# A list scheduler's walk, repeated backwards and forwards by latest times

## The chip, the cores and the metric

The kernel runs on one core of a Trainium2 chip. The metric is the device time of one execution in microseconds; less is better. The core has five engines that work side by side, each through its own queue in order: PE (TensorE, matmuls), DVE (VectorE), ACT (ScalarE), POOL (GpSimd) and SP (SyncE, which here issues all DMAs). An instruction that waits holds up everything behind it in its queue.

## The reference

Two stages, for x of shape (8, 4224, 192) and weights of shape (8, 4224, 8, 7).

```python
# 1: a causal convolution whose 7 taps are a softmax of weight_gen, per position and head (group = 24)
w = weight_gen - np.max(weight_gen, axis=-1, keepdims=True)
w = np.exp(w)
w = w / (np.sum(w, axis=-1, keepdims=True) + 1e-09)
x_pad = np.concatenate([np.zeros((B, 6, D)), x], axis=1)
x = np.einsum('bshk,bskhg->bshg', w, x_unf).reshape(B, S, D)     # x_unf: the 7 rows up to s, by head
# 2: Fourier mixing, layer norm, MLP 192 -> 768 -> 192
mixed = np.real(np.fft.fft(np.fft.fft(x, axis=1), axis=2))
u = x + mixed
un = (u - mean(u)) / np.sqrt(var(u) + 1e-06)
return u + np.maximum(un @ w_ch1, 0.0) @ w_ch2
```

## The kernel before

**Tiling.** A batch's 4224 rows are taken as 128 partitions by 33, in nine groups: eight of 4 rows a partition and one (number 8) of one row. Batch by batch the work goes through these stages, and the stages of one batch lie beside those of the next.

- *Convolution.* SP loads x (`x_sb`, L539) and the weights (`w`, L486). DVE and ACT make the softmax (maximum L488, difference L489, Exp on ACT L491, sum L493, L497, reciprocal L498, scaling L587/L594). DVE makes a product of x and one tap (`pr`, L656), and POOL adds it to `u` (L666). POOL makes a few products itself (L654). In batch 0, where PE has nothing else to do, the odd groups' products are added by PE in PSUM (`pa`, a matmul with the identity, L662), two taps of some groups are made by ACT (`wa` L616 on DVE, then L624 in pieces of 24 columns), and ACT copies the sum to `u` (L675). The products that PE adds take the three buffers of the tag `g2`, and the loads of `g` take the same buffers later.
- *First transform.* POOL folds `u` into `sm` (L680, L682), PE multiplies it (`pg`, L687), ACT copies one half (`up`, L693), DVE combines both (`gt`, L694, L697), SP writes it to DRAM (`g_d`, L700, L701).
- *Second transform.* SP reads it back in another layout (`g`, six loads a batch, L722), PE multiplies (`pp`, L732), ACT copies to `pq` (L736 to L746), PE multiplies again (`eo`, L761), ACT copies (`ot`, L766), DVE combines and adds to `u` (L767 to L771).
- *Norm.* Statistics on DVE (`bn`, `st`, L795, L796) or ACT (L800, L802), the reciprocal root `rs` (L804 to L811), the normalised `un` on ACT (L813), split into two fp16 halves `hl` (L821 on ACT, L822 and L824 on POOL or DVE), transposed by a DMA into `ht` (L830).
- *MLP.* PE multiplies with the first weights, split in fp16 halves too (`ph`, L855, five matmuls a block), ACT and DVE make the relu and its halves (`hh`, L861 to L866), PE multiplies with the second weights (`po`, L878; fp32 for the first seven groups, so that they need no split), DVE adds (L883), SP writes out (L887).
- *Preparation of the MLP's weights* w1 and w2 (rounding to fp16 halves and scales, L387 to L430, with two small matmuls `mr_w`, `me_w` L394, L397), with copies by SP (L456). Matmuls on data that are at hand (`warm_pp`, `warm_hl`, L709) stand in PE's queue where it would be idle.

**Order.** The code writes the instructions in one order, batch by batch with the stages interleaved. Before the program is compiled, `plan` sorts all five queues anew. It builds the graph of the instructions (who reads what another wrote, and which buffer of a tag each tile needs), gives each a busy time and a time to its end (`cost`), and walks: at each step it takes the lane that can issue earliest, and on it, of the instructions that can issue at that moment, the first in the written order. `HOP` is the time from an end on one engine to a start on the next. A tile takes a buffer when one of its tag's is spare, in the written order of the tiles. Then it links each queue's instructions into that order. These lines choose:

```python
at = [(t, k) for t, k in ((opens(k), k) for k in ks) if t is not None]
if at:
    now = max(free[lane], min(at)[0])
    if best is None or now < best[0]:
        best = now, lane, min(k for t, k in at if t <= now)
```

Of the kernel before, what the change touches and what calls it, by code (L numbers as in the profile page):

```python
# [12 lines left out]
F32 = mybir.dt.float32  # L13
# [11 lines left out]
DH = 97  # L25
# [26 lines left out]

LANES = {mybir.EngineType.PE: "pe", mybir.EngineType.DVE: "dve", mybir.EngineType.Activation: "act",
         mybir.EngineType.Pool: "pool", mybir.EngineType.SP: "sp"}
HOP = {"pe": 60, "dve": 33, "act": 33, "pool": 78, "sp": 26}
BYTES = {F32: 4, I32: 4, U32: 4, F16: 2}

# [12 lines left out]
def area(ap, kind):  # L70

    if kind == "psum":
        return (0, P), [(0, 1)]
    dims, base, parts, size = [list(d) for d in ap.ap], ap.offset, (0, 1), BYTES[ap.dtype]
    if kind != "dram":
        step, n = dims.pop(0)
        parts, base = ((base // step, base // step + n), base % step) if step else ((0, P), base)
    free, run = [], 1
    for step, n in dims:
        base += min(step, 0) * (n - 1)  # L80
        if n > 1 and step:
            free.append((abs(step), n))
    free.sort(reverse=True)
    while free and (free[-1][0] <= run or np.prod([n for _, n in free]) > 80):
        step, n = free.pop()
        run += step * (n - 1)
    spans = [base]
    for step, n in free:
        spans = [b + step * k for k in range(n) for b in spans]
    return parts, sorted((b * size, (b + run) * size) for b in spans)  # L90
# [18 lines left out]
def covers(a, b):  # L109

    (pa, sa), (pb, sb) = a, b
    return len(sa) == 1 and pa[0] <= pb[0] and pb[1] <= pa[1] and sa[0][0] <= sb[0][0] and sb[-1][1] <= sa[0][1]


def cost(ins, lane, reads, writes):

    count = lambda ap: int(np.prod([n for _, n in ap.ap[1:]]))
    out = writes[0]
    n = max(map(count, reads + writes))
    if lane == "pe":  # L120
        n = count(out)
        t = 2 * max(112 if 64 < n <= DH else 56, 0.846 * n) if reads[0].dtype == F32 else max(55.5, 0.4205 * n + 0.4)
        return t, t + 178
    if lane == "sp":
        if ins.opcode == "DmaTransposeAnt":
            return 1450, 2000 + 1.2 * n
        return 400, 2000 + WIRE * count(out) * BYTES[out.dtype]
    if lane == "dve":
        t = 150 + (6.27 if ins.opcode == "Reciprocal" else 1.042) * n + (60 if len(reads) == 3 and n < 512 else 0)
        return t - 83, t  # L130
    if lane == "pool":
        t = 183 + (1.92 if out.dtype == F16 else 2.13) * n
        return t - 45, t
    t = 190 + (0.833 if out.ap[-1][0] == 1 else 1.666) * n + 90 * (len(reads) - 1)
    return (t + 100, t + 90) if len(writes) > 1 else (t - 95, t)


def plan(nc, tc, homes, holds):

    ops, index = [], {}  # L140
    writers, readers, users = defaultdict(list), defaultdict(list), defaultdict(list)
    rows = defaultdict(list)
    for at, ins in enumerate(nc.cur_bb.bb.instructions):
        reads, writes = ([a.bass_ap for a in args if hasattr(a, "bass_ap")] for args in (ins.ins, ins.outs))
# [12 lines left out]
        for name, spot, w in spots:  # L157
            kind, tag, bufs = homes[name]
            if name not in users and bufs and kind != "dram":
                rows[kind, tag].append(name)  # L160
            users[name].append(k)
            if w and homes[name][0] != "psum":
                for old in (writers, readers):
                    old[name] = [(other, j) for other, j in old[name] if not covers(spot, other)]
            (writers if w else readers)[name].append((spot, k))
        for lo, hi, first in holds:
            if lo <= at < hi and first.engine == ins.engine:
                needs.setdefault(index[first.name], False)
        ops.append((ins, lane, cost(ins, lane, reads, writes), needs, {n for n, _, _ in spots}))

    after, left = defaultdict(list), [len(op[3]) for op in ops]
    for k, op in enumerate(ops):
        for j in op[3]:
            after[j].append(k)
    uses = {name: len(set(ks)) for name, ks in users.items()}
    ends, placed = defaultdict(float), set()
    spare = {row: [0.0] * homes[names[0]][2] for row, names in rows.items()}
    heads = {row: 0 for row in rows}
    ready = [0.0] * len(ops)
    free, waiting = ({lane: v for lane, v in zip(LANES.values(), vs)} for vs in ([0.0] * 5, [set() for _ in range(5)]))  # L180
    order = {lane: [] for lane in LANES.values()}

    def opens(k):

        t = ready[k]
        for name in ops[k][4]:
            row = homes[name][:2]
            if name in placed or row not in rows or not homes[name][2]:
                continue
            while rows[row][heads[row]] in placed:  # L190
                heads[row] += 1
            if rows[row][heads[row]] != name or not spare[row]:
                return None
            t = max(t, min(spare[row]) + HOP[ops[k][1]])
        return t

    for k, n in enumerate(left):
        if n == 0:
            waiting[ops[k][1]].add(k)
    table = None  # L200
    for _ in ops:
        best = None
        for lane, ks in waiting.items():
            at = [(t, k) for t, k in ((opens(k), k) for k in ks) if t is not None]
            if at:
                now = max(free[lane], min(at)[0])
                if best is None or now < best[0]:
                    best = now, lane, min(k for t, k in at if t <= now)
        now, lane, k = best
        ins, _, (busy, done), _, names = ops[k]  # L210
        if lane == "act":
            kind = str(getattr(ins, "func", "")).split(".")[-1]
            if kind in ("Exp", "Sqrt") and kind != table:
                now, table = now + 1283, kind
        waiting[lane].remove(k)
        order[lane].append(ins)
        free[lane], end = now + busy, now + done
        for name in names:
            row = homes[name][:2]
            if name not in placed:  # L220
                placed.add(name)
                if row in rows and homes[name][2]:
                    spare[row].remove(min(spare[row]))
            uses[name] -= 1
            ends[name] = max(ends[name], end)
            if not uses[name] and row in rows and homes[name][2]:
                spare[row].append(ends[name])
        for j in after[k]:
            to = ops[j][1]
            loose = to == lane and (lane == "pe" or not ops[j][3][k])  # L230
            ready[j] = max(ready[j], now if loose else end + HOP[to])
            left[j] -= 1
            if left[j] == 0:
                waiting[to].add(j)
    link = mybir.DependencyInfo(mybir.DependencyClass.NoSync, mybir.DependencyReason.DATA)
    for queue in order.values():
        for a, b in zip(queue, queue[1:]):
            tc.add_manual_dep(b, a.name, link, reason="plan")
    return max(ends.values())


def row_table():
# [45 lines left out]
def tile_dynconv_fnet_mlp(  # L288
# [693 lines left out]
    for b in range(B):  # L982
# [6 lines left out]
        for g in range(NG):  # L989
            if b > 0 or g >= QUICK:  # L990
                at = t0 - mix_at + step * g + (0.7 if b == 0 else 0)
                add(at, at + step, late_mix(g) if b == 0 and g >= QUICK else mix(b, g))
                add(max(at + step, t0 + g - 2.0), t0 + g - 1.0, norm(b, g))
    run()
    plan(nc, tc, homes, holds)


# [35 lines left out]
```

## Time and profile before

| | us |
|---|---|
| median of 3 runs | 1126.27 (1126.01 to 1127.51) |
| the profiled execution, its own time | 1124.56 |
| span of the profile, first to last instruction | 1122.8 |
| PE busy | 1077.9 (96%) |
| DVE busy | 969.8 (86%) |
| POOL busy | 876.7 (78%) |
| ACT busy | 817.8 (73%) |

The mean granted clock of PE is 0.983. "PEld" is the load of a matmul's stationary operand, which lies beside the matmuls. A row `waiter <- releaser: total, times, longest` gives the idle time of an engine and what ended it; "SPq" is an engine's queue at a DMA issue. In the chain, a row is the start, the length and the piece of work that was last to end. One execution alone is profiled; the page's fp32 matmuls count twice, since each is made in two passes.

### The profile page before, as it was taken

The numbers are of one execution on the slowest core, as the hardware profiler recorded it, in microseconds if no ns is written. First come the engines' busy times: TensorE is split into PE (matmuls) and PEld (weight loads), VectorE is DVE, ScalarE is ACT, GpSimd is POOL, SyncE is SP. The second block draws the span as 40 slices with busy tenths as digits, with TensorE's granted clock in tenths as the row PEclk, the third lists the DMA queues.
The fourth block names the chain that finished last, engine by engine and source line by source line (L and its number), as shares of the span: only waits on it lengthen the run. The fifth ranks groups of instructions, "written<-read, shape, count | busy, mean of one in ns | idle before, by whom it ended". The sixth has DMA issues, their size and how long they took to land.

```text
span 1122.8 us, 23426 instructions
## 1 busy us (share of the span) xinstructions
PE 1077.9 (96%) x8476; PEld 825.0 (73%) x8476; DVE 969.8 (86%) x1773; ACT 817.8 (73%) x2415; POOL 876.7 (78%) x759
## 2 busy tenths in 40 slices
PE   5986899999999999999999999999999999999998
PEld 2565487678777877787778877777778777787777
DVE  7987999779989999899999999899989999455543
ACT  4475766658986787778786888778787878689842
POOL 4979699699996999699997999599987999311200
PEclk9897799999999999999999999999999999999999
DMA  8334244533384246614474246623454222513321
GB/s 318 120 106 146 43 110 126 148 102 106 86 221 120 65 106 164 176 59 103 117 204 117 78 121 178 162 58 101 119 158 114 71 61 71 145 43 75 72 47 47
DMA packets 156500, 128.71 MB, mean 115 GB/s; under 512 B 108571, under 2 KB 133088, under 8 KB 156384
## 3 DMA queue, kind: packets, MB, share of 16 engines
q1 hardware_dynamic: 156384, 127.21, 41.6%
q8 instruction: 67, 1.10, 0.4%
q14 instruction: 49, 0.40, 0.1%
HBM read 61.46 MB, written 39.37 MB: 90 GB/s over the span
## 4 chain that ended last, share of the span: by engine, by line
PE 77%; DVE 10%; POOL 5%; issue 3%; ACT 3%; DMA 1%; SPq 0%; DVEq 0%; ACTq 0%; POOLq 0%
PE ph L855 33%; PE po L878 30%; PE eo L761 5%; PE pp L732 5%; POOL u L666 4%; PE pg L687 3%; DVE pr L656 3%; ACT pr L624 1%; PE pa L662 1%; DMA g<-g_d 1%; DVE u L666 1%; DVE u L656 1%; ACT w L491 1%; POOL sm L680 0%; DVE u L883 0%
## 5 line engine op out<-in xcount | busy, mean ns | idle before, releaser
L666 POOL TENSOR_TENSOR u<-u,pr 128x768 f32<-128x768 f32 (+1 forms) x396 | 655.5, 1673 | 53.5 <-DVE pr L656 46.2
L878 PE MATMUL po<-w2h,hh 128*128 128x192 f16 x2832 | 421.6, 246 | 0.0
L878 PEld LDWEIGHTS <-hh 128*128 128x128 f16 x4248 | 364.5, 98 | 68.2
L855 PE MATMUL ph<-ht,w1h 128*128 128x512 f16 (+1 forms) x1296 | 400.0, 363 | 3.0 <-ACT hh L861 1.5
L656 DVE TENSOR_TENSOR pr<-x_sb,wp 128x768 f32<-128x768 f32 (+1 forms) x415 | 354.0, 876 | 20.8 <-POOL u L666 16.4
L878 PE MATMUL po<-w2l,hh 128*128 128x192 f16 x1416 | 348.1, 246 | 0.0
L866 DVE SCALAR_TENSOR_TENSOR hh<-ph,hh 128x512 f16<-128x512 f32 (+1 forms) x390 | 245.1, 634 | 78.5 <-ACT hh L865 77.3
L855 PE MATMUL ph<-ht,w1l 128*128 128x512 f16 (+1 forms) x864 | 311.4, 363 | 0.0
L865 ACT ACTIVATE hh<-ph 128x512 f16<-128x512 f32 (+1 forms) x390 | 214.6, 553 | 118.7 <-PE ph L855 84.1
L855 PEld LDWEIGHTS <-w1h 128*128 128x128 f16 x1296 | 126.6, 99 | 85.8 <-DVE hl L824 2.3
L813 ACT ACTIVATE un<-u,rs 128x192 f32<-128x192 f32 x264 | 124.0, 535 | 26.6 <-POOL rs L811 21.3
L822 POOL TENSOR_TENSOR hl<-un,hl 128x512 f16<-128x512 f32 (+1 forms) x69 | 74.4, 1078 | 61.3 <-ACT hl L821 30.7
L855 PEld LDWEIGHTS <-w1l 128*128 128x128 f16 x864 | 85.7, 99 | 45.5 <-issue 3.3
L802 ACT ACTIVATE junk<-u,st 128x192 f16<-128x192 f32 x252 | 113.7, 451 | 3.8
L800 ACT ACTIVATE junk<-u 128x192 f16<-128x192 f32 x252 | 90.6, 360 | 25.3 <-DVE u L771 20.9
L761 PE MATMUL eo<-cs_sb,pq 97*128 97x97 f32 x544 | 90.8, 274 | 3.4 <-DVE u L771 3.4
L761 PEld LDWEIGHTS eo<-cs_sb,pq 97*128 97x128 f32 x544 | 83.5, 193 | 12.3 <-issue 3.6
L883 DVE SCALAR_TENSOR_TENSOR u<-po,isc,u 128x384 f32<-128x384 f32 (+1 forms) x122 | 72.7, 596 | 7.4 <-PE po L878 7.0
L680 POOL TENSOR_TENSOR sm<-u 128x382 f32<-128x382 f32 x64 | 64.3, 1005 | 7.5 <-ACT u L675 7.5
L811 POOL TENSOR_TENSOR rs<-st,rs 128x4 f32<-128x4 f32 (+1 forms) x69 | 15.4, 223 | 65.6 <-DVE rs L805 65.6
L736 ACT COPY pq<-pp 97x204 f32<-97x204 f32 (+1 forms) x96 | 46.5, 484 | 25.4 <-PE pp L732 24.2
L878 PE MATMUL po<-w2f,hh 128*128 128x192 f32 x336 | 63.8, 327 | 0.0
(108 smaller groups left out, 1295.5 us busy)
## 6 DMA issues: line engine op xcount, KB each, us to landing
out_dram<-u SPq DMA_DIRECT2D x64, 384.0 KB
x_sb<-in_x_dram SPq DMA_DIRECT2D x48, 384.0 KB
g<-g_d SPq DMA_DIRECT2D x40, 336.0 KB
x_sb<-in_x_dram SPq DMA_DIRECT2D x8, 864.0 KB
g_d<-gt SPq DMA_DIRECT2D x32, 195.0 KB
g_d<-gt SPq DMA_DIRECT2D x32, 189.0 KB
w<-in_weight_gen_dram SPq DMA_DIRECT2D x6, 924.0 KB
x_sb<-in_x_dram SPq DMA_DIRECT2D x8, 672.0 KB
```

Of the source, the lines that this page charges most:

```text
L656: last_product[b] = nc.vector.tensor_tensor(out=dst, in0=rows, in1=wk, op=ALU.mult)
L666: adder.tensor_tensor(out=u, in0=u, in1=pr, op=ALU.add)
L761: nc.tensor.matmul(eo[:, e, j, :], lhsT=pq[0:DH, e, r, r:r + P], rhs=cs_sb[:, e, :], start=True, stop=True)
L800: nc.scalar.activation(junk, uv[:, t, :], AF.Identity, scale=-1.0 / D, accum_out=st[:, t, 0:1])
L802: nc.scalar.activation(junk, uv[:, t, :], AF.Square, bias=st[:, t, 0:1], accum_out=st[:, t, 1:2])
L813: nc.scalar.activation(halves[t // 2][:, t % 2, :], uv[:, t, :], AF.Identity, bias=rs[:, 1, t:t + 1], scale=rs[:, 0, t:t + 1])
L822: lo_eng.tensor_tensor(out=hl[:, t0:t1, 2 * P:3 * P], in0=src[:, 0:t1 - t0, 0:P], in1=hl[:, t0:t1, 0:P], op=ALU.subtract)
L855: last_ph[n] = nc.tensor.matmul(ph[:, 0:T], lhsT=wt[:, cs_], rhs=ht[:, 0:T, blk], start=(i == 0), stop=(i == len(terms) - 1))
L865: nc.scalar.activation(a[:, 0:T], ph[:, 0:T], AF.Relu)
L866: nc.vector.scalar_tensor_tensor(out=l[:, 0:T], in0=ph[:, 0:T], scalar=0.0, in1=a[:, 0:T], op0=ALU.max, op1=ALU.subtract)
L878: nc.tensor.matmul(po[t // 2][:, t % 2, :], lhsT=hx[:, t], rhs=wx[:, c2, :], start=(c2 == 0 and i == 0), stop=(c2 == NH - 1 and i == len(t ...
L883: nc.vector.scalar_tensor_tensor(out=lt, in0=po[t // 2][:, 0:t % 2 + 1], scalar=scales[0][:, 1:2] if f32 else isc, in1=lt, op0=ALU.mult, o ...
```

## The change

`walk` is now a function over a rank and an order of the tiles, and can go back through the graph. First it walks forward with the written order as rank, as before. Then, up to three times (`TURNED`): it walks backwards from the end, those that ended last going first, with each tag's tiles taken in the order of their last use from behind; the time at which an instruction begins in that walk, counted from its total, is its latest time; then it walks forward again with the latest times as rank, once with these alone and once with 0.8 of them and 0.2 of the last start. The walk with the least total by the planner's own costs gives the order. Beside that, an unused buffer is open from −1000 ns instead of 0, PE's cost figures differ by some per cent, and where several instructions can issue at the same time the rank decides and not the written order. No instruction is added or removed: each queue holds the same ones. After the function `plan`, every line number is 17 higher.

```diff
+TURNED = 3
...
-        t = 2 * max(112 if 64 < n <= DH else 56, 0.846 * n) if reads[0].dtype == F32 else max(55.5, 0.4205 * n + 0.4)
+        t = 2 * max(112 if 64 < n <= DH else 56, 0.855 * n) if reads[0].dtype == F32 else max(55.8, 0.417 * n + 2.4)
...
-    spare = {row: [0.0] * homes[names[0]][2] for row, names in rows.items()}
...
+    def walk(rank, rows, back=False):
+
+        to, left = (before, after) if back else (after, before)
...
+        spare = {row: [-1e3] * homes[names[0]][2] for row, names in rows.items()}
...
+        for _ in ops:
+            at = [(max(free[lane], t), rank[k], k) for lane, ks in waiting.items()
+                  for t, k in ((opens(k), k) for k in ks) if t is not None]
+            if not at:
                 return None
...
+            now = min(at)[0]
+            lane = next(lane for lane in HOP if any(t == now and lanes[k] == lane for t, _, k in at))
+            k = min((r, k) for t, r, k in at if t == now and lanes[k] == lane)[1]
...
+        return max(end for _, end in span), span, order
+
+    best = now = walk(list(range(len(ops))), rows)
+    for _ in range(TURNED):
+        last = {name: max(now[1][k][1] for k in users[name]) for name in row_of}
+        turned = walk([-end for _, end in now[1]], {row: sorted(names, key=lambda name: -last[name]) for row, names in rows.items()}, True)
+        if turned is None:
+            break
+        late = [turned[0] - end for _, end in turned[1]]
+        now = min((w for w in (walk([part * t + (1 - part) * s for t, (s, _) in zip(late, now[1])], rows) for part in (1.0, 0.8)) if w),
+                  key=lambda w: w[0], default=None)
+        if now is None:
+            break
+        best = min(best, now, key=lambda w: w[0])
+    order = best[2]
```

What it moves, at the three places that the prediction speaks of. In the rows, a name is tile_batch_group and a number of its own; `pr_0_3_6` is batch 0, group 3, tap 6.

Place 1, POOL at the end of group 2's convolution of batch 0, before:

```order
L680 TENSOR_TENSOR sm_0_1_307<-u_0_1_210 128x2x191
L666 TENSOR_TENSOR u_0_2_222<-u_0_2_222,pr_0_2_6_302 128x768
L682 TENSOR_TENSOR sm_0_1_307<-u_0_1_210 128x2
L680 TENSOR_TENSOR sm_0_2_318<-u_0_2_222 128x2x191
L682 TENSOR_TENSOR sm_0_2_318<-u_0_2_222 128x2
L654 TENSOR_TENSOR pr_0_3_6_378<-x_sb_66,wq_0_3_331 128x768
L666 TENSOR_TENSOR u_0_4_335<-u_0_4_335,pr_0_4_1_382 128x768
```

and now:

```order
L697 TENSOR_TENSOR sm_0_1_307<-u_0_1_210 128x2x191
L699 TENSOR_TENSOR sm_0_1_307<-u_0_1_210 128x2
L671 TENSOR_TENSOR pr_0_3_6_378<-x_sb_66,wq_0_3_331 128x768
L683 TENSOR_TENSOR u_0_2_222<-u_0_2_222,pr_0_2_6_302 128x768
L683 TENSOR_TENSOR u_0_4_335<-u_0_4_335,pr_0_4_1_382 128x768
L697 TENSOR_TENSOR sm_0_2_318<-u_0_2_222 128x2x191
L699 TENSOR_TENSOR sm_0_2_318<-u_0_2_222 128x2
```

POOL's product of group 3 moved ahead of the last add and the folds of group 2. On DVE at the same place, before:

```order
L656 TENSOR_TENSOR pr_0_4_3_396<-x_sb_66,wp_0_3_328 128x768
L694 TENSOR_TENSOR gt_0_0_205<-pg_0_1_310,up1_80 128x2x97
L697 TENSOR_TENSOR gt_0_0_205<-pg_0_1_310,up1_80 128x2x95
L694 TENSOR_TENSOR gt_0_2_324<-pg_0_2_321,up0_79 128x2x97
L697 TENSOR_TENSOR gt_0_2_324<-pg_0_2_321,up0_79 128x2x95
L656 TENSOR_TENSOR pr_0_3_4_399<-x_sb_66,wp_0_3_328 128x768
L656 TENSOR_TENSOR pr_0_4_4_403<-x_sb_66,wp_0_3_328 128x768
```

and now:

```order
L673 TENSOR_TENSOR pr_0_4_3_396<-x_sb_66,wp_0_3_328 128x768
L673 TENSOR_TENSOR pr_0_3_4_399<-x_sb_66,wp_0_3_328 128x768
L673 TENSOR_TENSOR pr_0_4_4_403<-x_sb_66,wp_0_3_328 128x768
L673 TENSOR_TENSOR pr_0_3_5_422<-x_sb_66,wp_0_3_328 128x768
L673 TENSOR_TENSOR pr_0_4_5_426<-x_sb_66,wp_0_3_328 128x768
L673 TENSOR_TENSOR pr_0_4_6_431<-x_sb_66,wp_0_3_328 128x768
L711 TENSOR_TENSOR gt_0_0_205<-pg_0_1_310,up1_80 128x2x97
```

The four gt operations moved behind five products. PE's `pg` of group 2 moved behind four pairs of `pa` of group 3 as well.

Place 2, SP's queue between the two transforms of batch 0, before:

```order
L701 DMA g_d0_95<-gt_0_6_596 63x768
L456 DMA w1h1_89<-w1h_1_880 64x384 x3
L722 DMA g2_0_0_702<-g_d0_95 112x4x192
L722 DMA g2_0_4_720<-g_d0_95 112x4x192
L722 DMA g2_0_8_738<-g_d0_95 112x4x192
L456 DMA w1h1_89<-w1h_1_880 64x384
```

and now:

```order
L718 DMA g_d0_95<-gt_0_6_596 63x768
L739 DMA g2_0_0_702<-g_d0_95 112x4x192
L739 DMA g2_0_4_720<-g_d0_95 112x4x192
L739 DMA g2_0_8_738<-g_d0_95 112x4x192
L473 DMA w1h1_89<-w1h_1_880 64x384 x4
```

The first three loads of `g` moved ahead of the copies of `w1h`, which wait for ACT.

Place 3, DVE at the end of batch 1's convolution, where the products of batch 2 begin, before:

```order
L697 TENSOR_TENSOR gt_1_6_1899<-pg_1_7_1996,up1_80 128x2x95
L656 TENSOR_TENSOR pr_2_0_3_2140<-x_sb_66,wp_2_2058 128x768
L656 TENSOR_TENSOR pr_2_0_4_2174<-x_sb_66,wp_2_2058 128x768
L656 TENSOR_TENSOR pr_2_0_5_2204<-x_sb_66,wp_2_2058 128x768
L694 TENSOR_TENSOR gt_1_8_2044<-pg_1_8_2042,up0_79 128x97
L697 TENSOR_TENSOR gt_1_8_2044<-pg_1_8_2042,up0_79 128x95
```

and now:

```order
L714 TENSOR_TENSOR gt_1_6_1899<-pg_1_7_1996,up1_80 128x2x95
L673 TENSOR_TENSOR u_2_0_2070<-x_sb_66,wp_2_2058 128x768
L673 TENSOR_TENSOR pr_2_0_1_2073<-x_sb_66,wp_2_2058 128x768
L673 TENSOR_TENSOR pr_2_0_2_2109<-x_sb_66,wp_2_2058 128x768
L711 TENSOR_TENSOR gt_1_8_2044<-pg_1_8_2042,up0_79 128x97
L714 TENSOR_TENSOR gt_1_8_2044<-pg_1_8_2042,up0_79 128x95
```

Three products of batch 2 fewer stand ahead of batch 1's last gt. Two of the three splits of w2 (L430, now L447) moved behind it too.

More of the change, by code (lines that the diff above doesn't have):

```diff
@@ L169, in plan @@
         ops.append((ins, lane, cost(ins, lane, reads, writes), needs, {n for n, _, _ in spots}))
[L171 to L176, printed above, removed]
-    spare = {row: [0.0] * homes[names[0]][2] for row, names in rows.items()}
-    heads = {row: 0 for row in rows}
-    ready = [0.0] * len(ops)
@@ L180, in plan @@
[L180 to L192, printed above, removed]
-                return None
-            t = max(t, min(spare[row]) + HOP[ops[k][1]])
-        return t
@@ L197, in plan @@
[L197 to L222, printed above, removed]
-                    spare[row].remove(min(spare[row]))
[L224 to L234, printed above, removed]
@@ new lines, in plan, with opens @@
+    before, after = [op[3] for op in ops], [{} for _ in ops]
+    for k, needs in enumerate(before):
+        for j, sync in needs.items():
+            after[j][k] = sync
+    row_of = {name: row for row, names in rows.items() for name in names}
+    tiles = [[name for name in op[4] if name in row_of] for op in ops]
+    lanes = [op[1] for op in ops]
+    kinds = [str(getattr(op[0], "func", "")).split(".")[-1] if op[1] == "act" else "" for op in ops]
+    def walk(rank, rows, back=False):
+        to, left = (before, after) if back else (after, before)
+        left, ready, span = [len(n) for n in left], [0.0] * len(ops), [None] * len(ops)
+        uses = {name: len(set(users[name])) for name in row_of}
+        ends, placed, heads = defaultdict(float), set(), {row: 0 for row in rows}
+        spare = {row: [-1e3] * homes[names[0]][2] for row, names in rows.items()}
+        free, waiting = {lane: 0.0 for lane in HOP}, {lane: set() for lane in HOP}
+        order, table = {lane: [] for lane in HOP}, None
+        for k, n in enumerate(left):
+            if n == 0:
+                waiting[lanes[k]].add(k)
+        def opens(k):
+            t = ready[k]
+            for name in tiles[k]:
+                if name not in placed:
+                    row = row_of[name]
+                    while rows[row][heads[row]] in placed:
+                        heads[row] += 1
+                    if rows[row][heads[row]] != name or not spare[row]:
+                        return None
+                    t = max(t, min(spare[row]) + HOP[lanes[k]])
+            return t
+        for _ in ops:
+            at = [(max(free[lane], t), rank[k], k) for lane, ks in waiting.items()
+                  for t, k in ((opens(k), k) for k in ks) if t is not None]
+            if not at:
+                return None
+            now = min(at)[0]
+            lane = next(lane for lane in HOP if any(t == now and lanes[k] == lane for t, _, k in at))
+            k = min((r, k) for t, r, k in at if t == now and lanes[k] == lane)[1]
+            if kinds[k] in ("Exp", "Sqrt") and kinds[k] != table:
+                now, table = now + 1283, kinds[k]
+            waiting[lane].remove(k)
+            order[lane].append(ops[k][0])
+            busy, done = ops[k][2]
+            free[lane], end = now + busy, now + done
+            span[k] = now, end
+            for name in tiles[k]:
+                row = row_of[name]
+                if name not in placed:
+                    placed.add(name)
+                    spare[row].remove(min(spare[row]))
+                uses[name] -= 1
+                ends[name] = max(ends[name], end)
+                if not uses[name]:
+                    spare[row].append(ends[name])
+            for j, sync in to[k].items():
+                loose = lanes[j] == lane and (lane == "pe" or not sync)
+                ready[j] = max(ready[j], now if loose else end + HOP[lane if back else lanes[j]])
+                left[j] -= 1
+                if left[j] == 0:
+                    waiting[lanes[j]].add(j)
+        return max(end for _, end in span), span, order
@@ L238, in plan @@
             tc.add_manual_dep(b, a.name, link, reason="plan")
-    return max(ends.values())
+    return best[0]
 def row_table():
```

## The prediction

> **What bounds the kernel now.** I read the busy time by stretches of the span first, then the waits of each engine, the chain that ended last, and the timeline of the engines at the waits that mattered. Columns of the stretches: length, then busy time and instructions of PE, PEld, DVE, ACT and POOL, granted clock, DMA share, GB/s.
>
> ```profile
> 0.00:28.10 28.10, 14.19 (x39) 8.38 (x40) 20.93 (x44) 11.31 (x40) 12.38 (x21) 0.99 0.89 319
> 28.10:56.10 28.00, 25.58 (x70) 14.07 (x69) 25.89 (x38) 13.00 (x59) 26.85 (x20) 0.89 0.36 120
> 56.10:84.20 28.10, 24.88 (x103) 17.03 (x102) 25.20 (x57) 19.84 (x88) 20.52 (x18) 0.94 0.34 106
> 84.20:112.30 28.10, 17.20 (x122) 15.76 (x121) 21.18 (x61) 14.85 (x39) 28.10 (x18) 0.77 0.49 146
> 112.30:140.40 28.10, 22.89 (x103) 13.01 (x104) 27.91 (x65) 19.77 (x48) 18.58 (x15) 0.75 0.26 43
> 196.00:260.00 64.00, 59.34 (x369) 46.89 (x367) 51.09 (x84) 38.84 (x103) 54.19 (x45) 1.00 0.41 113
> 400.00:954.00 554.00, 554.00 (x4702) 428.49 (x4700) 529.75 (x947) 443.19 (x1288) 508.80 (x432) 1.00 0.44 117
> sum 1122.80, PE 1077.89 PEld 825.05 DVE 969.81 ACT 817.78 POOL 876.67; mean PE 107.79 PEld 82.50 DVE 96.98 ACT 81.78 POOL 87.67
> ```
>
> PE is idle for 1122.80 − 1077.89 = 44.9 us. From 400 to 954 it has no idle time at all. Its work is the same matmuls after the change, so a new order can take time away only where PE stands idle: 13.9 at the start, 2.4, 3.2, 10.9 and 5.2 in the next four rows, 4.7 between 196 and 260. It can give time back anywhere: DVE has 24 us left in the 554, POOL 45. These are the waits behind PE's idle time (total, times, longest):
>
> ```profile
> PE pa L662 <- DVE pr L656: 13.9, 4, 10.2
> PE warm_hl L709 <- DVE st L796: 6.6, 1, 6.6
> PE pp L732 <- DMA g<-g_d: 2.7, 1, 2.7
> PE eo L761 <- DVE u L771: 2.7, 1, 2.7
> PE ph L855 <- ACT hh L861: 1.5, 1, 1.5
> PE pp L732 <- DMA g<-g_d: 2.0, 3, 0.8
> ```
>
> The first is before 60 us, the next four from 60 to 130 (batch 0's mixing and norms), the last from 130 to 350 (batch 1's convolution and transform). Since PE is saturated behind, each microsecond by which the first MLP work starts earlier, or a later hole closes, comes off the end.
>
> **The change part by part.** No instruction is added or removed; all five queues are only sorted anew, so every term is a wait. The new cost figures of PE and the unused buffers that are open before time 0 have no price of their own; they act through that order, the latter at the start alone.
>
> *Start, 0 to 30 us.* PE's 10.2 us wait is for the first products, behind loads and the first softmax. SP now loads 864 KB of x ahead of the first weights instead of 672 KB: 192 KB at the 319 GB/s of the first row is 0.6 us later. Against that, DVE gets softmax pieces earlier, into holes of about 1.9 us in all. Bounds: 0.6 later to 1.9 earlier. I take **−0.3**, near the loads, as they come first.
>
> *Chunks 3 to 7 of batch 0.*
>
> ```profile
> 39.70 2.68 DVE L656 TENSOR_TENSOR pr<-x_sb,wp 128x768 f32<-128x768 f32 x3
> 41.82 1.48 POOL L654 TENSOR_TENSOR pr<-x_sb,wq 128x768 f32<-128x768 f32 x1
> 45.63 4.41 DVE L656 TENSOR_TENSOR pr<-x_sb,wp 128x768 f32<-128x768 f32 x5 [1.01 <-PE pa L662]
> 57.77 0.32 ACT up L693
> 73.48 0.34 ACT w L491
> 78.69 0.35 DVE L697 TENSOR_TENSOR gt<-pg,up 128x190 f32<-128x190 f32 x1
> ```
>
> DVE's five products at 45.63 wait for a buffer that PE frees when it has added POOL's product of 41.82, and PE's pg of chunk 2 stood ahead of that. POOL now makes this product before chunk 2's last add and folds, PE takes pg_2 four pairs of adds later, and four gt operations of DVE go behind the products. The products before ended at 42.38 (first row); so they start up to 45.63 − 42.38 = 3.25 earlier. Two gt operations (the last row's kind, 0.35, some 0.3 in the stream) still stand ahead of the next taps' weights, which takes 0.6 of it back: 2.65. ACT makes its taps from these weights and its chain runs on them until 73.48; three copies like that of 57.77 (0.27 each in the stream) move behind the taps: 0.8 more. Batch 0's last gt (78.69 and 0.35) comes **3.4** earlier. Ends: 0.8 if the buffer's release doesn't move, 4.1 if the gt operations cost nothing.
>
> *SP after that.*
>
> ```profile
> 79.42 0.31 SPq L701 DMA_DIRECT2D g_d<-gt  x1
> 82.56 1.78 SPq L456 DMA_DIRECT2D w1h<-w1h  x3
> 84.57 3.31 DMA g<-g_d
> 88.02 0.93 PE pp L732 x8
> 226.51 0.31 SPq L701 DMA_DIRECT2D g_d<-gt  x1
> 228.27 1.39 SPq L722 DMA_DIRECT2D g<-g_d  x3
> L709 PE MATMUL warm_pp<-gt,ident x40: 275/275/550, 79.2 to 85.0; 128*128 128x128 f32 x40
> ```
>
> SP stood at L456 until 82.56, when ACT had w1h ready, and the loads of g, issued at 84.57, were queued behind it. Now they stand ahead. What they then wait for is the write of g_d: in batch 1 SP issues it at 226.51 and the loads at 228.27, so about 1.76 after. That puts them at 81.2 here, 3.4 earlier; landed 3.31 after, 84.5. But the 20 warm-up matmuls stand ahead of pp on PE and end at 85.3 (85.0 and 0.275). So pp starts at 85.3 instead of 88.02, **−2.6** (2.7 less a step of release), the wait of 2.7 above. The w1h copies that now come later go into the MLP's weights and have 30 us until its first matmul. Three loads of x now pass two of the earlier g_d writes on SP; those have some 20 us before the last write, which is the one that pp waits for, so I cost them at nothing; without that cover each costs its issue, 0.3 as in the row of 79.42. With the 3.4, pp is 6.0 earlier.
>
> *Mixing and norms, 95 to 125 us.*
>
> ```profile
> 104.53 0.46 DVE w2f L424
> 112.84 0.62 DVE bn L795 x2
> 123.28 0.50 ACT hh L861
> ```
>
> DVE is the chain here. Two preparations of w2 such as that at 104.53 go behind the norms (0.9 earlier for u of the first groups), while the statistics of group 2 now go ahead of the first hl (0.62 and three short ones of 0.08: 0.85 later). One split of w1 on the way is also later, 0.5 as an estimate from 104.53's row. Net **+0.5**, ends −0.9 and +1.5. The first relu at 123.28 stood behind a normalisation on ACT, PE's 1.5 us wait; it now stands ahead: **−1.5**. MLP work of batch 0 so gets −0.3 − 3.4 − 2.6 + 0.5 − 1.5 = **−7.3**. No ph waits for a transposed ht in the wait table, so the groups that follow have some lead there.
>
> *Batch 1's convolution and transform, 186 to 232 us.*
>
> ```profile
> 206.15 3.10 DVE L430 SCALAR_TENSOR_TENSOR w2l<-w2f,sc_w,w2h 128x384 f16<-128x384 f32 x3
> 223.21 2.59 DVE pr L656 x3
> 225.97 0.16 DVE gt L697
> 226.22 1.46 PE L878 MATMUL po<-w2f,hh 128*128 128x192 f32 x8
> 227.53 0.38 PE L855 MATMUL ph<-ht,w1h 128*128 128x512 f16 x1
> 228.60 1.46 PE L878 MATMUL po<-w2f,hh 128*128 128x192 f32 x8
> 232.57 0.91 PE L732 MATMUL pp<-te_sb,g 102*97 102x102 f32 x8 [0.45 <-DMA g<-g_d]
> ```
>
> PE's first pp of batch 1 started at 232.57 after a wait of 0.45, 6.4 after the last gt (225.97 and 0.16). In the new order two blocks of five ph matmuls (227.53 to 228.60: 1.07 each) and eight po (four take 227.53 − 226.22 = 1.31), 4.8 us in all, no longer stand ahead of it. So PE asks for it at 232.1 − 4.8 − 7.3 = 220.0. The last gt would have to be done at 213.6, 12.5 earlier than it was. What I find for it: convolution 1 restarts behind batch 0's norms, 7.3 − 1.5 = 5.8 earlier but for w2's preparations that now stand there (0.9) and a softmax step that waits for ACT behind the norms (some 0.9, a guess): 4; of the three splits of w2 on DVE (3.10) two go behind the gt and the third behind the softmax of batch 2, which gives 3.1 and takes 0.9 back; the three products of 223.21 go behind the gt, 2.6; hl of group 7 goes behind the folds on POOL. The DVE terms and the restart sum to 8.8; POOL's lies beside them. PE then waits 12.5 − 8.8 = 3.7 instead of the 2.0 in the wait table: **+1.7**. Ends: a last gt 5 or 12 us earlier gives +5.5 or −1.5.
>
> *From 260 us.* PE's queue has the same kind of work and no holes; norm steps on POOL come later. I take 0, bounded below by a rival.
>
> Sum: −7.3 + 1.7 = −5.6. The profiled execution took 1124.56 (its span 1122.8 and 1.8 around it), 1.7 below the median of 1126.27; the difference is made on it, giving 1119.0, and against the median 1120.7. I forecast **1120.7**.
>
> **Rivals.** *The gain is given back at batch 1's pp.* If the last gt comes only 5 earlier, PE waits 7.5 there, and −7.3 + 5.5 = −1.8 is left: 1124.5; with the late convolution as the bound for all that follows it can be no better than that gt. For it: POOL is busy for 54.19 of the 64 us there, DVE for 51.09, so the convolution may be bound on POOL. Against it: the moved products are plain. With its own bounds it covers 1122.5 to 1125.6.
>
> *A larger front.* Full closing of the buffer wait (4.1), the start's 1.9 and a last gt 12 earlier give −7.3 − 0.7 − 1.6 − 1.5 = −11.1: 1115.2. The clock belongs here:
>
> ```profile
> 123.10:126.54 3.44, 2.72 (x7) 0.50 0.21 48
> 126.54:130.00 3.46, 3.46 (x21) 1.00 0.42 81
> ```
>
> The mean clock is 0.77 and 0.75 in the two stretches there; it was half up to 126.54 and came back right after a window of 3.44 us in which PE was busy for 2.72. Without the 1.5 us relu wait the window ahead could be as full, which frees the clock one window earlier: 1.7 us of matmul time, 1119.0. I give that 2 in 10 and leave it out of the sum, since the wait of 6.6 that halves the clock stays. [...]
>
> *Slower.* The new order holds an op back until it is late by the planner's own latest times. In the 554 us row DVE is 96% and POOL 92% busy, so one step that slips waits long: if in each of batches 1 to 7 the first MLP matmul of a group finds its hl behind one more add, that costs
>
> ```profile
> L666 POOL TENSOR_TENSOR u<-u,pr 128x768 f32<-128x768 f32 (+1 forms) x396 | 655.5, 1673 | 53.5 <-DVE pr L656 46.2
> ```
>
> 1.67 each, 11.7 in all, less 5.6: +6.1, 1132.4. It decides from (5.6 + 2.25) / 7 = 1.1 a batch on. Against it: PE waited nowhere there, so some lead exists.
>
> *The order does nothing*: the front's gain is lost since batch 0's MLP waits on the transposes: 1126.3 within 0.2%.
>
> **How the numbers follow.** 0.2% is 2.25 us, about what a measurement of this kernel can tell from no change. My forecast with its bounds, 1117.5 to 1122.5, has 0.50; given back 0.20 (half of it below 1124.0); larger front 0.14; slower 0.10; nothing 0.06. Faster: 0.50 + 0.13 + 0.14 = 0.77; same 0.13; slower 0.10. The range 1113.5 to 1125.6 leaves out the slower case and little else.
>
> **What the profile after would show.** Right: the g loads of batch 0 issue about 1.8 us after the g_d write, ahead of w1h; pp of batch 0 at about 82; DVE's five products of chunk 3 directly behind those before; no wait ph on hh near 117; PE's total idle near 39. Wrong: a wait pp on g of more than 6 us near 220, any wait of ph on ht from 260 on, or PE idle in the stretch from 400 to 954.

## The result, and the profile after

| | before | after |
|---|---|---|
| median, us | 1126.86 (1126.01 to 1127.51) | 1118.07 (1116.87 to 1119.48) |
| ratio | | 0.9923, 95% interval 0.9910 to 0.9935 |
| profiled execution, its own time | 1124.56 | 1118.23 |
| span | 1122.8 | 1116.5 |
| mean granted clock | 0.983 | 0.989 |

The forecast was 1120.7, range 1113.5 to 1125.6. The medians differ by 8.8 us, the two profiled executions by 6.3. Later runs of the kernel before lie between 1123.9 and 1130.7 with mean clocks from 0.985 down to 0.977, so the execution that was profiled (1124.56) was among its faster ones, 2.3 to 2.9 below the medians; positions in the traces below are against that one.

The stretches of the kernel after, with the columns of the prediction:

```profile
0.00:28.10 28.10, 16.77 (x46) 9.58 (x47) 22.39 (x45) 11.51 (x40) 14.60 (x23) 1.00 0.94 318
56.10:84.20 28.10, 24.59 (x126) 18.25 (x125) 25.07 (x60) 17.61 (x72) 22.37 (x18) 0.94 0.55 154
112.30:140.40 28.10, 26.79 (x141) 18.41 (x142) 26.97 (x50) 17.85 (x41) 20.22 (x16) 0.94 0.18 36
196.00:260.00 64.00, 63.14 (x464) 53.75 (x462) 56.36 (x97) 45.04 (x126) 56.52 (x49) 1.00 0.37 95
260.00:400.00 140.00, 136.64 (x1130) 104.21 (x1130) 130.59 (x234) 111.45 (x330) 126.89 (x109) 0.99 0.48 126
400.00:954.00 554.00, 552.62 (x4695) 427.59 (x4694) 524.27 (x939) 439.93 (x1272) 504.73 (x436) 1.00 0.45 116
sum 1116.50, PE 1072.53 PEld 822.33 DVE 964.13 ACT 820.37 POOL 875.80; mean PE 107.25 PEld 82.23 DVE 96.41 ACT 82.04 POOL 87.58
```

PE was idle for 4.7 us from 196 to 260 and is now idle for 0.9. But from 260 to 400 it is idle for 3.4 (1.5 before), and for 1.4 between 400 and 954, where it had none. In the whole span its idle time hardly changed: 1116.50 − 1072.53 = 44.0, against 44.9. Its busy time fell by 5.4, for the same 8476 matmul passes; the section on the prediction comes back to it. PE's waits (from 60 to 130, and the first row from 130 to 350):

```profile
PE ph L872 <- DMA ht<-hl: 3.9, 2, 3.3
PE warm_hl L726 <- DVE rs L822: 7.1, 1, 7.1
PE pp L749 <- DMA g<-g_d: 3.8, 2, 2.5
PE ph L872 <- DVE hl L841: 2.5, 1, 2.5
PE eo L778 <- DVE u L788: 1.9, 1, 1.9
```

The wait of ph on a relu is gone; ph on ht is new (two waits, one of 3.3), and ph on hl in batch 0 grew from 1.3 to 2.5. Since the matmuls are the same, the start of a named one in both traces tells where the time went. This is the difference in us, less is earlier (first column: its start before); the columns with e-numbers are experiments that follow; e3's profiled execution took 1136.37, the longest of its seven:

| first matmul of | before at | after | e2 | e3 | e4 | e7 | e9 | e12 |
|---|---|---|---|---|---|---|---|---|
| warm_pp, batch 0 (after the last gt) | 79.19 | −6.52 | −6.25 | +1.72 | −5.59 | −5.50 | −5.69 | −6.39 |
| pp, batch 0 | 88.02 | −7.74 | −7.23 | +1.85 | −6.41 | −2.78 | −6.77 | −7.22 |
| eo, batch 0 | 101.12 | −6.00 | −5.65 | +1.91 | −6.46 | −2.48 | −6.81 | −8.96 |
| ph, batch 0, group 0 | 119.97 | −6.36 | −6.00 | +1.55 | −5.66 | −2.28 | −6.01 | −8.45 |
| ph, batch 0, group 1 | 133.28 | −8.75 | −8.39 | +1.86 | −7.77 | −1.37 | −8.13 | −11.21 |
| eo, batch 1 | 244.63 | −13.03 | −11.72 | +3.70 | −4.71 | −0.94 | −12.71 | −15.49 |
| ph, batch 1, group 3 | 311.65 | −12.88 | −10.32 | +3.21 | −5.05 | −1.05 | −12.84 | −15.31 |
| ph, batch 1, group 4 | 324.83 | −9.57 | −10.10 | +6.30 | −5.14 | −1.17 | −12.95 | −15.42 |
| ph, batch 1, group 5 | 338.25 | −7.86 | −10.10 | +9.18 | −5.14 | −1.17 | −12.66 | −15.05 |
| ph, batch 2, group 0 | 397.38 | −8.85 | −9.93 | +8.18 | −4.97 | −1.04 | −13.66 | −16.05 |
| ph, batch 7, group 8 | 1110.56 | −6.75 | −10.10 | +11.45 | −5.14 | −1.25 | −11.03 | −15.96 |

So the new order gains 13 us up to batch 1's transform and gives half of it back afterwards. The first batch's work comes earlier through the softmax at the start, the products of groups 3 and 4 (the prediction's chunk 3) and SP's queue. DVE at the start, of before and then of after:

```profile
18.33 1.55 DVE L489 TENSOR_TENSOR w<-w,wm 128x1344 f32<-128x1344 f32 x1
21.27 1.56 DVE L493 TENSOR_REDUCE wm<-w 128x192 f32<-128x1344 f32 x1 [0.72 <-ACT w L491]
36.23 0.95 DVE L656 TENSOR_TENSOR pr<-x_sb,wp 128x768 f32<-128x768 f32 x1
```

```profile
14.46 1.55 DVE L506 TENSOR_TENSOR w<-w,wm 128x1344 f32<-128x1344 f32 x1
18.10 1.55 DVE L510 TENSOR_REDUCE wm<-w 128x192 f32<-128x1344 f32 x1
34.08 0.95 DVE L673 TENSOR_TENSOR pr<-x_sb,wp 128x768 f32<-128x768 f32 x1
35.81 8.73 DVE L673 TENSOR_TENSOR pr<-x_sb,wp 128x768 f32<-128x768 f32 x10
```

The subtraction of batch 0's long softmax now runs 3.9 earlier, and Exp on ACT is done without DVE waiting for it. The run of products that 36.23 opens in the kernel before opens at 34.08 here, 2.15 earlier. The ten products in one row belong to groups 3 and 4: the five that had waited for a buffer follow without a hole, and the last ends at 44.54 instead of 50.04. Then the last gt, from the chain that ended last (after; start, duration):

```profile
72.35 0.26 DVE gt L714
72.98 3.53 DMA g_d<-gt
83.58 5.30 DMA g<-g_d
```

And SP's timeline beside it:

```profile
76.78 1.39 SPq L739 DMA_DIRECT2D g<-g_d  x3
78.22 2.69 SPq L473 DMA_DIRECT2D w1h<-w1h  x4
80.98 2.50 SPq L473 DMA_DIRECT2D w1l<-w1l  x4
83.58 3.28 SPq L739 DMA_DIRECT2D g<-g_d  x3
```

The first three loads do stand ahead of w1h, but the write of g_d took 3.53, not 1.76. The DMA share was 0.44 in these 3.53 us and 0.20 in batch 1's 1.76. The second three loads now stand behind eight copies: that is the wait of 2.5 for g.

### The profile page after: what moved, and what is told of

Its sections match the earlier page's. It is cut to its first block, busy times and chain, and to the rows that moved or that the text cites. A ratio compares the mean times of both kernels' runs of the same rounds, so it can differ in the third digit from the quotient of the medians.

```text
span 1116.5 us, 23468 instructions
## 1 busy us (share of the span) xinstructions
PE 1072.5 (96%) x8476; PEld 822.3 (74%) x8476; DVE 964.1 (86%) x1773; ACT 820.4 (73%) x2415; POOL 875.8 (78%) x759
## 4 chain that ended last, share of the span: by engine, by line
PE 66%; POOL 10%; DVE 9%; issue 5%; DMA 3%; ACT 2%; SPq 0%; DVEq 0%; ACTq 0%; POOLq 0%
PE ph L872 28%; PE po L895 26%; POOL u L683 8%; PE pp L749 5%; PE eo L778 4%; DVE pr L673 3%; PE pg L704 2%; DMA g<-g_d 1%; DVE hh L883 1%; POOL sm L697 1%; PE pa L679 1%; DMA ht<-hl 1%; DMA g_d<-gt 1%; ACT un L830 1%; DVE u L673 1%
## 5 line engine op out<-in xcount | busy, mean ns | idle before, releaser
L883 DVE SCALAR_TENSOR_TENSOR hh<-ph,hh 128x512 f16<-128x512 f32 (+1 forms) x390 | 247.9, 638 | 80.2 <-ACT hh L882 79.6
L830 ACT ACTIVATE un<-u,rs 128x192 f32<-128x192 f32 x264 | 127.6, 536 | 31.5 <-POOL rs L828 23.3
L778 PE MATMUL eo<-cs_sb,pq 97*128 97x97 f32 x544 | 88.1, 271 | 2.1 <-DVE u L788 1.9
```

The source lines that it names most:

```text
L778: nc.tensor.matmul(eo[:, e, j, :], lhsT=pq[0:DH, e, r, r:r + P], rhs=cs_sb[:, e, :], start=True, stop=True)
L830: nc.scalar.activation(halves[t // 2][:, t % 2, :], uv[:, t, :], AF.Identity, bias=rs[:, 1, t:t + 1], scale=rs[:, 0, t:t + 1])
L883: nc.vector.scalar_tensor_tensor(out=l[:, 0:T], in0=ph[:, 0:T], scalar=0.0, in1=a[:, 0:T], op0=ALU.max, op1=ALU.subtract)
```

## The experiments

In each, all times are against runs of the kernel before that were made beside them on the same chip (medians 1127.3 to 1127.5).

**e1: is it the walk?**

```diff
-TURNED = 3
+TURNED = 0
```

> The changed kernel with TURNED = 0: one forward walk by the written order, but with the new cost figures of PE, with unused buffers open early and with the new rule for ties. At the two places of batch 0 (POOL's product of group 3, the loads of g on SP) its order is that of before. Theory (the latest times make the gain): 1126.9 within 2 us. Rival (the cost figures and the buffers make a good part of it): 1122 or less.

Measured: 1128.51, ratio 1.0014 (1.0004 to 1.0024). The cost figures, the early buffers and the rule for ties make no gain by themselves; the turned walks make it. Turned walks with the old cost figures were not tried.

**e2, e3, e4: which stretch of the order gains and which loses.** The two orders are joined: first the one up to a cut, then what is left of the instructions in the order of the other. The lines below are e2's; e3 swaps the two orders, and e4 cuts at `ph_0_1_0_`.

```diff
+    cut = next(i for i, k in enumerate(first) if any(n.startswith("ph_1_2_0_") for n in ops[k][4]))
+    done = set(first[:cut])
+    seq = first[:cut] + [k for k in then if k not in done]
```

> The new order up to the first MLP block of group 2 of batch 1 (about 284 us), and from there the instructions that are left in the order of before. PE is 12.9 us ahead of the kernel before at that point in the new kernel's trace, and only 8.9 ahead at 400 us and 6.75 at the end. Theory A (what is lost after 300 us is lost by the new order there): PE stays 11 to 13 ahead, 1114 to 1116. Rival B (PE that is early runs into the norms and the convolution, which DVE and POOL can't deliver sooner, whatever the order): 1118 to 1120, and PE waits on ht or pg between 300 and 400 us here too.

> The order of before up to the same block (about 297 us there), and the new order from there. Theory A (loss by the new order after 300 us): 1130 to 1133. Rival B (loss only since PE is early): 1126 to 1128.

> The new order up to the first MLP block of group 1 of batch 0 (about 124 us; PE is 8.75 ahead there in the new kernel's trace), and the order of before for the rest. Theory (batch 1's convolution and transform gain on their own by their new order, 4 more us at 247): 8.75 are left at 124, the old order then waits at batch 1's pp as I worked out: 5 to 8 us gain, 1119 to 1122. Rival (the start of batch 0 is worth all of it, the rest of the old order keeps it): 1117 to 1118, or below if the new order after 300 us loses what this one doesn't.

Measured: e2 1114.40 (0.9886, 0.9869 to 0.9904); e3 1131.59 (1.0049, 1.0031 to 1.0066); e4 1119.14 (0.9923, 0.9908 to 0.9938). Theory A holds both ways: without the late part of the new order 3.7 us more are gained, and with it alone the kernel becomes slower by 4.3. In the table, e3 loses 3.1 at the same matmul as the new kernel, group 4 of batch 1, although PE is not early there. e2 loses 1.9 at its cut instead: it is 12.2 ahead at group 2 of batch 1 and 10.3 at group 3. e4 against e2 is worth 4.7: batch 1's convolution and transform gain by their own order, since with the old one e4's lead falls from 7.8 to 4.7.

**e5: is the split of hl the cause?** POOL between 300 and 307 in the new kernel, where batch 1's group 4 gets its hl in two pieces, with two adds and a fold between them:

```profile
300.83 1.19 POOL L839 TENSOR_TENSOR hl<-un,hl 128x512 f16<-128x512 f32 x1
306.61 0.69 POOL L841 TENSOR_TENSOR hl<-un,hl 128x256 f16<-128x256 f32 x1
```

```diff
+    for b in range(1, 8):
+        for g in range(9):
+            pair = [k for k in seq if lanes[k] == "pool" and has(k, "hl_%d_%d_" % (b, g))]
+            if len(pair) == 2:
+                seq.remove(pair[1])
+                seq.insert(seq.index(pair[0]) + 1, pair[1])
```

> The changed kernel, with the second piece of each hl on POOL put right behind its first, in batches 1 to 7 (the new order splits them in 21 groups; at 302 us two adds and a fold, 4.6 us, stand between, and PE then waits 3.3 us for ht). Theory (what is lost after 300 us is this split): PE keeps 12 us or more, 1114 to 1115.5, no wait of ph on ht. Rival (the split only happens to lie there, the late part of the order loses elsewhere, at g or at the products): 1117 to 1119.

Measured: 1120.12 (0.9933, 0.9919 to 0.9947), no better than the new kernel. My theory fell: hl was done at 304.86, but PE still waited 2.9 for this ht. SP's timeline in e5, and the transfer in its chain:

```profile
305.32 3.13 SPq L652 DMA_DIRECT2D x_sb<-in_x_dram  x4
308.61 0.33 SPq L599 DMA_DIRECT2D w<-in_weight_gen_dram  x1
309.11 4.29 SPq L943 DMA_TRANSPOSE ht<-hl  x1
```

```profile
309.11 8.25 DMA ht<-hl
```

The transpose waited in SP's queue behind four x loads and a w load, and then took 8.25 us. So an earlier hl alone gains nothing; what it would gain with the queue clear was not tried.

**e9: the transpose ahead of the loads.** In the new order of SP these loads had moved ahead of it; before, they stood behind it. The same two views of the new kernel, and then the edit, as SP's queue before and after it:

```profile
303.11 3.13 SPq L556 DMA_DIRECT2D x_sb<-in_x_dram  x4
306.39 0.33 SPq L503 DMA_DIRECT2D w<-in_weight_gen_dram  x1
307.32 4.04 SPq L847 DMA_TRANSPOSE ht<-hl  x1
```

```profile
307.32 7.89 DMA ht<-hl
```

```diff
 DMA out_0_dram<-u_1_1
+DMA_TRANSPOSE ht_1_4<-hl_1_4
 DMA x_sb<-in_x_dram 128x768 x3
 DMA x_sb<-in_x_dram 128x576
 DMA w_4<-in_weight_gen_dram 128x1848
-DMA_TRANSPOSE ht_1_4<-hl_1_4
```

> The changed kernel with one transpose moved on SP: that of batch 1's group 4 goes ahead of the three x loads of 384 KB, the one of 288 KB and the w load of 924 KB that the new order put ahead of it (in the order of before it stood ahead of them). Its hl is done at 307.3 either way. In the new kernel it is issued at 307.32 and lands 7.9 us later. Theory (the loads slow the transpose down, and that is the 3.3 us wait): it lands after 3.6 to 4.5, PE waits 0 to 0.5 for ht, 3 us are kept: 1115 to 1116. Rival (the late hl is the cause, the loads are not): the wait stays above 2, 1117.5 to 1119.

Measured: 1114.07 (0.9884, 0.9869 to 0.9900), 4.0 below the new kernel. SP's timeline and PE's wait in e9:

```profile
307.31 1.44 SPq L942 DMA_TRANSPOSE ht<-hl  x1
308.84 2.26 SPq L651 DMA_DIRECT2D x_sb<-in_x_dram  x4
```

```profile
PE ph L967 <- DMA ht<-hl: 0.7, 1, 0.7
```

Issued at the same time as in the new kernel, it holds SP for 1.44 instead of 4.04. PE no longer waits at this group; the 0.7 is another ht wait that the new kernel has too. The gain is more than the 3.3 us of the wait. Two stretches of PE in the new kernel, then the second one in e9 (length, PE busy, clock, DMA share, GB/s):

```profile
311.99:315.40 3.41, 0.15 (x2) 1.00 1.15 273
315.40:318.82 3.42, 3.42 (x15) 0.50 0.63 203
```

```profile
315.40:318.82 3.42, 3.42 (x30) 1.00 0.94 335
```

In the stretch after the wait the clock is at 0.50, and PE gets 15 passes done where e9 gets 30 in the same 3.42 us: 1.7 us more, as an estimate from these two rows. In the table the new kernel loses 5.0 from group 3 to group 5 (−12.88 to −7.86) and e9 0.2. So this one place of one queue costs most of the 6.3 that the late order gives back: 4.0 by the medians. In the kernel before, the transpose of group 5 stands behind four x loads and a w load too, and holds SP for 3.68 from 320.18. PE does not wait for it: it needs it at 338.25, 18 us later, where the new kernel needed its own 4 to 5 us after the issue.

**e6 and e7: the front's terms by themselves.** e6 is the kernel before with the three g loads moved, e7 the new order up to the first warm-up matmul, with the old order of SP behind it (w1h first).

```diff
 DMA g_d0<-gt_0_6
+DMA g2_0_0, g2_0_4, g2_0_8 <-g_d0
 DMA w1h1<-w1h_1
-DMA g2_0_0, g2_0_4, g2_0_8 <-g_d0
```

> The kernel before, with the first three loads of g of batch 0 ahead of the w1h copies on SP and nothing else. My term: pp starts 2.7 earlier, bounded by the warm-up matmuls, 1124.5 against 1127.2. Rival (the g_d write lands only 4 us after its issue, as in the new kernel's trace, where it took 3.5): pp 1 to 1.5 earlier and part of it lost again to the second three loads, 1126 to 1127.

> The new order up to the first warm-up matmul of batch 0 (72.7 us in the new kernel), the order of before from there, its SP order with w1h ahead of the loads of g included. Theory (the start and chunks 3 to 7 are worth 6.4 us at the last gt and the rest of batch 0's gain is their passing on): the last gt at 72.6, a gain of 5 to 6.5, 1121 to 1122. Rival (SP's wait on w1h takes it back, since w1h doesn't come earlier): 1124 to 1127.

Measured: e6 1125.61 (0.9984, 0.9972 to 0.9995), e7 1122.37 (0.9960, 0.9947 to 0.9972). SP's timeline in e6, then in e7, and PE's wait in e7:

```profile
80.08 0.31 SPq L809 DMA_DIRECT2D g_d<-gt  x1
83.49 1.39 SPq L830 DMA_DIRECT2D g<-g_d  x3
```

```profile
74.00 0.33 SPq L804 DMA_DIRECT2D g_d<-gt  x1
79.31 1.78 SPq L559 DMA_DIRECT2D w1h<-w1h  x3
81.32 1.47 SPq L825 DMA_DIRECT2D g<-g_d  x3
```

```profile
PE pp L835 <- DMA g<-g_d: 6.8, 1, 6.8
```

In e6 the loads come 3.4 after the write, 1.1 earlier than before, and pp only 0.67 earlier: the trace is the rival's of the expectation, while the median lies between its two ranges. In e7 the last gt is early by 5.5, but w1h is not ready before 79.31, and PE waits 6.8 for g: 2.7 of the 5.5 are lost at once. By the medians e7 gains 5.1 (just outside the theory's range) and e6 1.9, together 7.0; e4, which has both and the rest of the new order up to 124 us, gains 8.1. That the two are worth more together than one by one is therefore likely, but not clear of the intervals.

**e8: the second three loads too.** e2 with all seven loads of batch 0's g ahead of the copies.

```diff
+    seq = behind(seq, 'sp', lambda k: has(k, 'g2_0_'), lambda k: has(k, 'gt_0_6_', 'g_d0'))
```

> The kernel of e2 (new order to 284 us, then that of before, 1114.4) with the second three loads of g of batch 0 ahead of the w1h and w1l copies too. In the new kernel they are issued at 83.58 behind eight copies, land at 88.9, and PE waits 2.5. Theory (SP's queue is what makes them late): eo 1.5 to 2.5 earlier, 1112 to 1113. Rival (they wait for their buffers, which pp frees at 82 to 86): 1114 to 1114.5.

`behind` puts the picked instructions of SP right behind the last write of g_d. Measured: 1112.26 (0.9865, 0.9850 to 0.9880), 2.1 below e2; the intervals of the two overlap (0.9869 to 0.9880), so this gain is likely and not shown. In the traces, first pp to first eo takes 13.0 instead of 14.7, as the theory has it, but the two profiled executions end within 0.1 of each other.

**e10 and e11: the clock.** PE kept busy between the last eo and the first ph.

```diff
-            keep_warm(("ph", 3), f"hl{g}", hl[:, 0, 0:P], hl[:, T - 1, 0:2 * D], WARM[2])
+            keep_warm(("ph", 3), f"hl{g}", pq[0:DH, 0, 1, 1:1 + P], cs_sb[:, 0, :], BUSY)    # BUSY = 26
```

> The kernel before, in which the 12 warm-up matmuls on hl of batch 0's group 0 are replaced by 26 on data that are ready (pq and the DFT matrix, 97 columns), so that PE works on between the last eo at 107.6 and the first ph at 120.0; nothing else moves. The result doesn't use them. Theory (the half clock from 106 to 126.5 costs time on the first ph): the clock is back at 113 to 116, the first ph block takes half as long, 1124 to 1126. Rival (relu and norms set the pace there, the clock doesn't matter): 1126.9 to 1128.

> The kernel of e8 (1112.3) with the same 26 matmuls in place of the 12. If the clock still costs something in front of and in the first ph block (the clock was half from 100 to 112 and for a part of 113 to 118 in the new kernel): 1110.5 to 1111.5. If not: 1112 to 1113.

Measured: e10 1128.71 (1.0012, 1.0003 to 1.0021), e11 1115.06 (0.9890, 0.9877 to 0.9904; e8 was 1112.26). Four stretches of e10 (length, PE busy, clock, DMA share, GB/s):

```profile
109.47:112.88 3.41, 3.41 (x18) 0.50 0.00 0
112.88:116.30 3.42, 3.42 (x18) 0.50 0.10 20
116.30:119.71 3.41, 3.35 (x16) 0.50 0.50 95
126.54:129.95 3.41, 3.41 (x12) 0.51 0.39 75
```

The edit did not do what it was meant to: PE was busy with hardly a break and the clock stayed at half, longer than before (to 129.9 instead of 126.5). e11 lies outside both ranges of its expectation, 2.8 above e8. What the clock costs on the first ph is not shown by these two.

Other traces do show it. e5 has the new kernel's order on all five engines up to 288 us, and its first eo starts at the same time (94.94 against 95.12), but its clock went another way. From 90.60 to 121.36 in e5, then in the new kernel (length, PE busy, clock, DMA share, GB/s):

```profile
90.60:121.36 30.76, 19.66 (x75) 0.50 0.27 75
```

```profile
90.60:121.36 30.76, 18.60 (x96) 0.73 0.27 76
```

The first ph of group 1 starts at 127.54 in e5 and at 124.53 in the new kernel. Four executions have this order: from eo to that ph the new kernel, e2, e9 and e5 take 29.4, 29.4, 30.8 and 32.6 us, of which the clock was at half for 13.7, 13.7, 17.1 and 26.4.

**e12: what the runs point to, together.** The new order up to batch 2's first ph, the old one from there, e8's seven loads, e9's transpose.

> What the runs so far point to, in one kernel: the new order up to the first MLP block of batch 2 (about 388 us), the order of before from there, the seven loads of g of batch 0 ahead of the w1h and w1l copies (as in e8), and the transpose of batch 1's group 4 ahead of the loads (as in e9). Theory (each is worth what it was alone: 1114.1 with the transpose, 2 for the loads of g, 1.5 to 2.5 for what e9's order loses after 388 us): 1109.5 to 1111.5. Rival (the hand-over from one order to the other costs the 2 us that it cost in e2): 1112 to 1113.

Measured: 1108.85 (0.9834, 0.9820 to 0.9848), 18.5 below the kernel before, 9.2 below the new one, and a little below the theory's range. No cost of the hand-over shows here. Two of its stretches:

```profile
260.00:400.00 140.00, 140.00 (x1175) 107.19 (x1174) 134.59 (x242) 114.28 (x343) 129.93 (x112) 1.00 0.48 132
400.00:954.00 554.00, 554.00 (x4717) 429.44 (x4716) 522.29 (x937) 437.93 (x1263) 503.04 (x436) 1.00 0.44 117
```

PE has no idle time from 260 to 954. What the late order still loses after 388 us (2.6 in e9's column) is gone with the old order there (0.1 in e12's); which of its instructions lose it was not taken apart.

## Why the prediction was right, and where not

The direction was right, and the size lies in the range: 8.8 by the medians and 6.3 by the two traces, 5.6 forecast. That the traces come so near is luck. The front came out at −8.75 (−7.3 forecast), batch 1's transform at −4.3 (+1.7) and the stretch from 260 us at +6.3 (0): two errors of about 6 us cancelled. In the traces:

- *Where time can come from:* the prediction let a new order take time away only where PE stands idle, and expected 39 us of idle time. That step failed: idle time is 44.0 after 44.9, and the busy time of the same matmuls fell by 5.4. In the kernel before, the clock was at half for 37.5 us of the profiled execution, all of it before 127 us, and PE was busy for 27.5 of them; in the new one it was for 23.9, and PE was busy for 16.8. In the rows at 315.40 (the new kernel and e9) 15 passes at half clock take as long as 30 at the full one; taken for all of them, half of the difference of the busy times is 5.35, so by this estimate the clock accounts for all of the 5.4. (It is an account and not yet a cause: where nothing waits for PE, a shorter matmul only makes a longer wait.) The four runs of the new kernel have mean clocks from 0.986 to 0.989, those of the kernel before 0.977 to 0.985, so this comes with the order. The prediction had the clock in its rivals alone.
- *Start:* forecast −0.3, measured −2.15 at the products of 34.08, outside the bounds. The first adds come 0.46 later, as the loads say, but the long softmax 3.2 earlier: I took the nearer end of the range, and the holes on DVE were the term.
- *Chunks 3 to 7:* forecast −3.4. The mechanism is as described: ten products in one row, whose last ends 5.50 earlier, so the closed hole is worth 3.35 beside the start's 2.15 (3.25 expected). The last gt is 6.43 earlier in all (5.5 at the matmul behind it in e7), so 4.3 are left for this term, just over its upper end.
- *SP:* forecast −2.6 on top. pp gained 1.3 more than the last gt. The step that failed is the wait for the g_d write: 1.76 in batch 1, 3.5 here, with the DMAs busier (0.44 against 0.20). And what the prediction left out, the second three loads of g behind eight copies, took 1.7 back (eo −6.00 after pp −7.74).
- *Mixing and norms:* forecast +0.5 and −1.5. From eo to the second ph the lead grows by 2.75. The relu wait went as described, and the clock came back sooner (0.94 instead of 0.75 from 112.3 to 140.4). By the four executions above, the new order with 20.5 us at half, as in the kernel before, would take about 31.5 where that took 32.2. So, as an estimate from these rows, 2 of the 2.75 are the clock's and 0.7 the order's, where 1.0 was forecast. The *larger front* put the half clock down to PE's wait of 6.6; in the trace before the clock is at 0.50 from 106.06 and that wait begins at 108.05. The fuller window that it let bring the clock back came in the new kernel: PE is busy for all of 114.00 to 117.41, at 0.50, and the clock is at 1.00 behind it. In e10 three such stretches from 109.47 to 119.71, busy for 3.35 of 3.41 and more, are followed by 0.50 again.
- *Batch 1's transform:* forecast +1.7, measured −4.3. This term had the wrong sign. I had the last gt 8.8 earlier; it is 14.7 earlier, and no wait for it is left at pp:

```profile
211.14 0.25 DVE L714 TENSOR_TENSOR gt<-pg,up 128x95 f32<-128x95 f32 x1
217.95 0.87 PE L749 MATMUL pp<-te_sb,g 102*97 102x102 f32 x8
```

  Each moved piece (the three splits, the three products) was there, but I let the convolution restart only 4 earlier, by a guess. DVE's first u of batch 1 is 6.0 earlier (128.1 to 122.1), and the convolution gains on its way, for which the prediction had no term: its gt are 7.1 earlier at 147 us and 10.0 at 201, before any of the moved pieces comes. The holes at mr_w and me_w, which I kept, shrank too (2.7 to 0.5).
- *From 260 us:* forecast 0, measured +6.3. This is the other step that failed, and it is the *slower* rival at a smaller size: something held back until it is late. Two of the signs of being wrong came, a wait of ph on ht and PE idle between 400 and 954. I looked for it on POOL, in hl behind the adds; the split was there, but e5 shows that closing it gains nothing. e9 shows that SP's loads ahead of a transpose cost 4, in a wait of 3.3 and in the half clock behind it. It happened at one place, not in seven batches.

The rival "given back at batch 1's pp" did not come. The "larger front" did: its clock at the first ph, and a last gt of batch 1 that came earlier still than it assumed. In the chances, half of the 0.20 of "given back" was counted as 0.13 in the sum for "faster"; it should have been 0.10.

## What to carry to other kernels

When an order is planned by a model, look at what the model leaves out. Here `cost` gives each DMA a time by its own size alone, so a transpose behind 2.4 MB of loads took 7.89 us and the plan still called it in time; and it has no clock, while a wait of 3.3 us on PE, with the half clock behind it, cost 5.0. Do not take PE's idle time for all that an order can win or lose: look at the granted clock too. Compare the start of the same matmul in both traces along the span: it shows at once which stretches of a new order gain and which lose, and joining two orders at a cut tests it. Before a gain is called shown in a trace, compare it with the medians: e7 is 1.25 ahead at the end of its trace and 5.1 faster by the medians.

## What the runs showed of the hardware that I had not expected

The DMA transpose of batch 1's group 4 was slow where SP issued it right behind four x loads and one of w: it held SP for 4.04 us in the new kernel and 4.29 in e5, and PE could go on 7.89 and 8.25 after its issue; with the same loads behind it (e9), it held SP for 1.44. What makes it slow was not tried.

In the new kernel at 312 to 319 us a wait of PE cost more than its length: 3.3 us of wait, and 1.7 us more in the 3.42 behind it, where the clock was at 0.50.

In e10 the clock stayed at 0.50 through 52 passes of fp32 matmuls of 97 columns, without a gap from 107.9 to 119.2. In the kernel before it was at 0.50 in the stretch in which the warm-up matmuls of 128 columns began (79.19) and at 1.00 in the next:

```profile
78.75:82.16 3.41, 2.98 (x14) 0.50 0.40 114
82.16:85.58 3.42, 3.15 (x28) 1.00 0.18 44
```

What tells the two kinds of matmul apart was not tried.
